# A transformer block on one core: the down projections of chunks 0 and 1 as one Strassen pair

## Chip, cores and metric

The kernel runs on one core of one Trainium2 chip. The metric is the device time of the whole kernel in microseconds, from inputs in DRAM to the output in DRAM. A core has a matrix engine (TensorE, "PE" in the profile), VectorE ("DVE"), ScalarE ("ACT"), GpSimd ("POOL"), and a queue engine that issues most transfers (SyncE, "SP"). Matmul results land in PSUM, from where VectorE or ScalarE copies them out.

## What is computed

The input x has 2048 rows of 1024. A pre-norm block with sliding, dilated attention is followed by a pre-norm block with a bilinear feed-forward of width 3584. All weights and the output are bfloat16.

```
h  = x + A(layernorm(x))
out = h + B(layernorm(h))

A(y): q, k, v = split(y @ wqkv)              # 32 heads of 32
      logits[s, w] = q[s] . k[s - 2w] / sqrt(32),  w = 0..7, masked where s - 2w < 0
      o = softmax(logits) weighted sum of v[s - 2w]
      return o @ wo
B(y): g = y @ w_gate;  u = y @ w_up          # 1024 -> 3584
      return (g * u) @ w_down                # 3584 -> 1024
```

## The kernel before

The 2048 rows are handled in four chunks of 512. First come q, k and v of all chunks. The attention itself runs on VectorE, as a background generator whose steps are laid between the other work: a step's instruction is placed when the estimated time of the matmuls has paid for it. Attention output goes through DRAM to be turned around (`oD` to `od` to `oT`), then the output projection `wo`, the second norm and the feed-forward follow.

Chunks 2 and 3 already share Strassen products: their gate/up in pair blocks, and their down projection with the four quarters of a 1024 x 3584 by 3584 x 1024 product (two chunks by two halves of the features, two halves of the features by two halves of the columns). Strassen's form takes seven block products in place of eight, with sums of blocks in float16, and needs the values scaled: a power of two from a sum of absolute values of all of a tensor ("row sums", taken on ScalarE and totalled by one small matmul).

Before the change chunk 0's down projection is a plain one, and chunk 1's is a Strassen product by itself, its rows halved (256 rows per block):

```python
psum = ctx.enter_context(tc.tile_pool(name="psum", bufs=8, space=PSUM))   # eight banks, in turn
...
def ffn2(c, hf, hT, hs, between={}):                                      # chunk 0, plain
    acc = [psum.tile([128, 512], F32, tag="mm", ...) for t in range(4)]
    for b in range(4):
        for j in range(7):
            f = b * 7 + j
            for t in range(4):
                nc.tensor.matmul(acc[t][:], lhsT=hT[f][:, bass.ts(t, 128)], rhs=wts["wd", c, hf, b][:, j, :], ...)
            if c == 0:
                abs_sum_down(hf, b, j)          # row sum of 128x512 down weights, on ScalarE
            bg.step(0.86)                        # lets the attention go on
...
def dprod(ps, q, lhs, rhs, fresh, lo=0, n=TC):                             # 14 matmuls
    for k in range(NP):
        nc.tensor.matmul(ps[...], lhsT=lhs[k][:, bass.ts(q, 128)], rhs=rhs[k][...], ...)
...
nxt = wo_ln2(0)                  # output projection and norm of chunk 0
qkv(3, range(4, 6), last=True)   # v of chunk 3
start_attention(3)
lnT2, hs = nxt
hT = ffn1(0, lnT2)               # gate/up of chunk 0: 7 blocks of 8 groups
bg.finish(atts[1])
nxt = wo_ln2(1)                  # output projection and norm of chunk 1 (norm on VectorE)
for hf in range(2):
    ffn2(0, hf, hT, hs)
lnT2, hs = nxt
hT = ffn1(1, lnT2, ...)          # gate/up of chunk 1
... # chunk 1's down projection: seven products of two dprods (28 matmuls), wo of chunks 2 and 3 between them
... # 14 pair blocks: gate/up of chunks 2 and 3; then their down projection
```

In `ffn1` a group is eight matmuls into one bank; ScalarE copies gate (`gs`) and up (`us`) out of PSUM, VectorE multiplies them, ScalarE takes row sums:

```python
mm_group(pg, wts["wg", c, b], j, lnT);  nc.scalar.copy(gs[:], pg[:]);  bg.step(GROUP_US)
mm_group(pu, wts["wu", c, b], j, lnT);  nc.scalar.copy(us[:], pu[:])
nc.vector.tensor_tensor(gs[:], gs[:], us[:], ALU.mult)
abs_sum(c, b, j)
```

At the end of one chunk's attention, GpSimd's queue moves the output:

```python
nc.gpsimd.dma_start(od[c].rearrange("c g d s -> (c g) d s"), oD[:])
oT = att.tile([128, KO, 4, SUB], BF, tag="oT", name=f"oT{c}")
for cp in range(4):
    nc.gpsimd.dma_start(oT[:, :, cp, :], od[c][cp].rearrange("(hg hl) d s -> (hl d) hg s", hl=4))
```

Of the kernel before, what the change touches and what calls it, by code (L numbers as in the profile page):

```python
# [78 lines left out]
def kernel(  # L79
# [41 lines left out]

    bg = Background()
# [13 lines left out]
    def stream_wd(c, hf):  # L136
        for b in range(4):
            stream.append((("wd", c, hf, b), wd_v[:, bass.ts(b, 7), bass.ts(hf, 512)], 7))

    NH = NF // 4  # L140
    for c in range(2):
        stream_wo(c)
        if c > 0:
            stream_wd(0, 0)
            stream_wd(0, 1)
        for b in range(7):
            stream.append((("wg", c, b), wg_v[:, :, bass.ts(b, 512)], KO))
            stream.append((("wu", c, b), wu_v[:, :, bass.ts(b, 512)], KO))
    def stream_down(name, e, hf, halves):
        for a in halves:  # L150
            stream.append((("dn", name, a), wd_e[e][:, bass.ts(a, 7), bass.ts(hf, 512)], 7))

    stream_down("21", 1, 0, (0, 1))
    stream_down("11", 0, 0, (0, 1))
    stream_wo(2)
    stream_down("12", 0, 1, (0,))
# [100 lines left out]
    class NormOnScalar(Norm1):  # L257

        def sums(self):
            room = small.tile([128, 4, 4], F32, tag="nroom", name=f"nroom{self.c}")  # L260
            self.s, self.nm, self.ss, self.nb = (room[:, i, :] for i in range(4))
            junk = lnp.tile([128, D], BF, tag="ln", name=f"njunk{self.c}")
            xs = xtiles[self.c]
            for t in range(4):
                nc.scalar.activation(junk[:], xs[t][:], ACTF.Copy, accum_out=self.s[:, t:t + 1])
                yield "later", GROUP_US
            nc.scalar.activation(self.nm, self.s, ACTF.Copy, scale=-1.0 / D)
            for t in range(4):
                nc.scalar.activation(junk[:], xs[t][:], ACTF.Square, bias=self.nm[:, t:t + 1],
                                     accum_out=self.ss[:, t:t + 1])  # L270
                yield "later", GROUP_US
# [4 lines left out]

        def rows(self):
            for t in range(4):
                ln = lnp.tile([128, D], BF, tag="ln", name=f"ln{self.c}_{t}")
                nc.scalar.activation(ln[:], xtiles[self.c][t][:], ACTF.Identity, bias=self.nb[:, t:t + 1],  # L280
                                     scale=self.rs4[:, t:t + 1])
                self.lns[t] = ln
                self.transpose(t)
                yield "later", GROUP_US
# [158 lines left out]

    def attention(c):
        qD, kD = qkv_in["q", c], qkv_in["k", c]
        lg = att.tile([128, W, SUB], F32, tag="lg", name=f"lg{c}")
        for wp in range(W // 2):
# [14 lines left out]
            yield 1.0  # L462
        if c == 0:
            nc.vector.tensor_tensor(lg[0:32, :, 0:16], lg[0:32, :, 0:16], mask[:], ALU.add)
# [54 lines left out]
    def wo_ln2(c):  # L519
# [8 lines left out]
        for t in range(4):  # L528
            for hf in range(2):
# [12 lines left out]
                bg.spend(0.7)  # L542
                bg.step(GROUP_US)
        norm(3)
        retire(2)
        return lnT, hs
# [35 lines left out]
    scale_gu, scale_d, scale_h = Scale("gu", 56), Scale("d", 56), Scale("h", 56)  # L582
    scale_h1 = Scale("h1", 28)

    def abs_sum(c, b, j):
        wt = wts["wg" if c == 0 else "wu", c, b]
        junk = lnp.tile([128, 2, 512], BF, tag="ln", name=f"junk{c}_{b}_{j}")
        scale_gu.add(28 * c + 4 * b + j, wt[:, bass.ts(j, 2), :], junk[:])

    def abs_sum_down(hf, b, j):  # L590
        junk = lnp.tile([128, 512], BF, tag="ln", name=f"junkd{hf}_{b}_{j}")
        scale_d.add(28 * hf + 7 * b + j, wts["wd", 0, hf, b][:, j, :], junk[:])
# [5 lines left out]
    def abs_sum_h1(f, ht):  # L598
        junk = lnp.tile([128, TC], BF, tag="ln", name=f"junke{f}")
        scale_h1.add(f, ht[:], junk[:])  # L600

    def ffn1(c, lnT, at={}):
        hT = []
        for b in range(7):
            if b == 5 and c + 1 < NCH:
                hss[c + 1] = load_x(c + 1, "h", nc.sync)
            for j in range(4):
                pg = psum.tile([128, TC], F32, tag="mm", name=f"pg{c}_{b}_{j}")
                mm_group(pg, wts["wg", c, b], j, lnT)
                gs = t1k.tile([128, TC], BF, tag="t1k", name=f"gs{c}_{b}_{j}")  # L610
                nc.scalar.copy(gs[:], pg[:])  # L611
                bg.step(GROUP_US)
                pu = psum.tile([128, TC], F32, tag="mm", name=f"pu{c}_{b}_{j}")
                mm_group(pu, wts["wu", c, b], j, lnT)
                us = t1k.tile([128, TC], BF, tag="t1k", name=f"us{c}_{b}_{j}")
                nc.scalar.copy(us[:], pu[:])  # L616
                nc.vector.tensor_tensor(gs[:], gs[:], us[:], ALU.mult)  # L617
                abs_sum(c, b, j)
                bg.spend(0.45)
                bg.step(GROUP_US)  # L620
                hT.append(gs)
                if (b, j) in at:
                    at[b, j]()
                f = len(hT) - 3
                if c == 1 and f >= 0:
                    abs_sum_h1(f, hT[f])
# [3 lines left out]
        if c == 1:  # L630
            for f in range(NF - 2, NF):
                abs_sum_h1(f, hT[f])
        return hT

    def ffn2_store(c, t, hf, acc, hs, lo=0, n=512):
        cols = bass.ds(hf * 512 + lo, n)
        nc.vector.tensor_tensor(hs[t][:, cols], acc[:], hs[t][:, cols], ALU.add)
# [520 lines left out]
```

## Time and profile before

| | |
|---|---|
| time, median of three runs | 776.8 us (776.63 to 778.61) |
| profiled span | 775.2 us |
| granted TensorE clock | 1.00 |
| TensorE / VectorE / ScalarE / GpSimd busy | 769.3 / 605.3 / 484.0 / 142.1 us |
| moved by DMA | 134.38 MB, mean 173 GB/s |
| stages by TensorE's clock | q, k, v to 163.6; wo of chunk 0 to 177.4; v of chunk 3 to 191.2; gate/up 0 to 287.9; wo of chunk 1 to 301.7; down 0 to 350.0; gate/up 1 to 446.8; down 1 with wo of 2 and 3 to 516.8; pair blocks and the last down projection to 775.2 |

How to read it: the page gives each engine's busy time, its busy share in 40 slices of the span (one digit each, tenths), the chain of waits followed back from the last instruction, and groups of instructions with their mean durations. Answers of the trace give timelines (start and length in us, then engine, source line, operation, output and inputs, and in brackets how long the engine stood idle before it and what ended that) and the waits of one engine. A matmul's duration in the trace overlaps the next one's; from start to start is what counts.

### The profile page before, as it was taken

To read this page: it belongs to the slowest core of one execution; us is meant where nothing else is said; L and a number is where in the kernel's file an instruction comes from. 1 tells how busy PE (TensorE), PEld (TensorE's weight loads), DVE (VectorE), ACT (ScalarE), POOL (GpSimd) and SP (SyncE) were. 2 spreads that over 40 slices of the span, in tenths; PEclk is the share of its full clock that TensorE was granted. 3 is DMA by queue.
4 is the path that set the end of the run, shared out by engine and by line. 5 is a ranking of instruction groups with operands and counts; after the bars stand their busy time and mean duration, and the time that the engine had idled before them with its cause. 6 is when DMAs were issued, how large, how long until landed. Compare 5 with 4: busy or idle time off the path is not lost.

```text
span 775.2 us, 10420 instructions
## 1 busy us (share of the span) xinstructions
PE 769.3 (99%) x3691; PEld 353.5 (46%) x3691; DVE 605.3 (78%) x766; ACT 484.0 (62%) x1040; POOL 142.1 (18%) x152
## 2 busy tenths in 40 slices
PE   8999999999999999999999999999999999999998
PEld 6444444444444444444444444444444444444444
DVE  5639999999999989999979859985553444578863
ACT  4639564322866662965777899746677776788240
POOL 0000000200002000011000001008778687600000
PEclk9999999999999999999999999999999999999999
DMA  8998896997947964978445592644332423740001
GB/s 278 265 260 199 157 230 151 299 271 224 310 133 236 308 235 125 288 257 277 142 143 192 182 299 68 157 98 114 109 95 69 109 59 106 240 140 28 0 28 55
DMA packets 183716, 134.38 MB, mean 173 GB/s; under 512 B 81264, under 2 KB 176496, under 8 KB 181616
## 3 DMA queue, kind: packets, MB, share of 16 engines
q1 hardware_dynamic: 176912, 110.12, 50.9%
q0 software_dynamic: 3584, 22.02, 8.9%
q10 hardware_dynamic: 3168, 1.57, 0.8%
q8 instruction: 29, 0.48, 0.3%
q14 instruction: 23, 0.19, 0.1%
HBM read 104.86 MB, written 22.02 MB: 164 GB/s over the span
## 4 chain that ended last, share of the span: by engine, by line
PE 93%; DVE 3%; DMA 2%; ACT 1%; issue 0%; ACTq 0%; DVEq 0%
PE ps L411 20%; PE pg L411 12%; PE pu L411 12%; PE dx L807 6%; PE pz L700 6%; PE acc L646 6%; PE py L700 6%; PE px L700 6%; PE wo L532 4%; PE wo L852 4%; PE pv L700 3%; PE dy L807 3%; PE ex L807 2%; DMA lnT<-lnr 1%; DMA w_qkv<-in_A_wqkv_dram 1%; PE ps L372 1%
## 5 line engine op out<-in xcount | busy, mean ns | idle before, releaser
L411 PE MATMUL ps<-lnT,w_qkv 128*128 128x512 bf16 x736 | 159.5, 379 | 0.0
L411 PEld LDWEIGHTS <-w_qkv 128*128 128x128 bf16 x736 | 71.9, 98 | 86.2
L411 PE MATMUL pu<-lnT,w_wu 128*128 128x512 bf16 x448 | 105.8, 379 | 0.0
L411 PE MATMUL pg<-lnT,w_wg 128*128 128x512 bf16 x448 | 105.8, 379 | 0.0
L324 ACT CAST sg<-ps 128x512 bf16<-128x512 f32 x96 | 55.2, 585 | 52.3 <-PE ps L411 49.2
L451 DVE TENSOR_TENSOR prod<-qD,kD 128x4096 bf16<-128x4096 bf16 x32 | 72.4, 2285 | 12.8 <-DMA kD<-kd 12.7
L494 DVE TENSOR_TENSOR pv<-vD,at 128x4096 bf16<-128x4096 bf16 x32 | 72.5, 2285 | 0.3
L700 PEld LDWEIGHTS <-sw 128*128 128x128 f16 x448 | 43.8, 98 | 53.8 <-issue 1.2
L411 PEld LDWEIGHTS <-w_wu 128*128 128x128 bf16 x448 | 43.8, 98 | 52.9
L411 PEld LDWEIGHTS <-w_wg 128*128 128x128 bf16 x448 | 43.7, 98 | 52.8
L616 ACT CAST us<-pu 128x512 bf16<-128x512 f32 x56 | 33.0, 590 | 43.0 <-PE pu L411 41.8
L700 PE MATMUL px<-lnT,ws 128*128 128x512 bf16 x224 | 55.2, 379 | 0.0
L700 PEld LDWEIGHTS <-ws 128*128 128x128 f16 x336 | 32.9, 98 | 39.7
L506 POOL DMA_DIRECT2D od<-oD x4 | 2.2, 542 | 264.3 <-DVE oD L504 264.3
L646 PE MATMUL acc<-w_wd,gs 128*128 128x512 bf16 x224 | 48.5, 379 | 0.0
L681 POOL TENSOR_TENSOR sw<-ws 128x512 f16<-128x512 f16 x26 | 30.0, 1152 | 85.1 <-PE py L700 77.8
L611 ACT CAST gs<-pg 128x512 bf16<-128x512 f32 x56 | 32.6, 583 | 12.9 <-PE pg L411 10.6
L453 DVE TENSOR_TENSOR prod<-prod 128x4096 bf16<-128x4096 bf16 x16 | 36.6, 2289 | 0.4
L560 ACT ACTIVATE junkd<-w_wd 128x512 bf16<-128x512 bf16 x56 | 34.3, 613 | 0.0
L646 PEld LDWEIGHTS <-gs 128*128 128x128 bf16 x224 | 21.9, 98 | 26.4
L617 DVE TENSOR_TENSOR gs<-gs,us 128x512 bf16<-128x512 bf16 x56 | 23.5, 419 | 12.5 <-ACT us L616 12.5
L185 ACT ACTIVATE rs<-mv,eps 128x1 f32<-128x1 f32 (+1 forms) x21 | 6.2, 297 | 42.0 <-DVE mv L182 36.6
(321 smaller groups left out, 1391.5 us busy)
## 6 DMA issues: line engine op xcount, KB each, us to landing
w_wg<-in_B_w_gate_dram SPq DMA_DIRECT2D x14, 1024.0 KB, 6.7
w_wu<-in_B_w_up_dram SPq DMA_DIRECT2D x14, 1024.0 KB, 5.4
w_wd<-in_B_w_down_dram SPq DMA_DIRECT2D x8, 896.0 KB, 6.2
w_pair<-in_B_w_gate_dram SPq DMA_DIRECT2D x14, 512.0 KB, 4.0
w_pair<-in_B_w_up_dram SPq DMA_DIRECT2D x14, 512.0 KB, 5.2
w_wo<-in_A_wo_dram SPq DMA_DIRECT2D x6, 1024.0 KB, 6.2
w_qkv<-in_A_wqkv_dram SPq DMA_DIRECT2D x5, 1024.0 KB, 11.0
kd<-sg SPq DMA_DIRECT2D x32, 144.0 KB, 3.3
```

What stands on the lines that cost most here:

```text
L324: nc.scalar.copy(sg[:, HB:HB + TC], ps[:])
L411: nc.tensor.matmul(ps[:], lhsT=wt[:, ko, bass.ts(j, 128)], rhs=rhs[:, ko, :], start=(ko == 0), stop=(ko == KO - 1))
L451: nc.vector.tensor_tensor(prod[:, j], qD[:], kD[:, :, o:o + SUB], ALU.mult)
L453: nc.vector.tensor_tensor(prod[:, :, 0:16], prod[:, :, 0:16], prod[:, :, 16:32], ALU.add)
L494: nc.vector.tensor_tensor(pv[:, j], vD[:, :, o:o + SUB], at[:, w, None, :].to_broadcast((128, DH, SUB)), ALU.mult)
L532: nc.tensor.matmul(ps[:], lhsT=oTs[c][:, kk, t, :], rhs=wts["wo", c, hf][:, kk, :], start=(kk == 0), stop=(kk == KO - 1))
L560: nc.scalar.activation(junk, src, ACTF.Abs, accum_out=self.l1[:, k:k + 1])
L611: nc.scalar.copy(gs[:], pg[:])
L616: nc.scalar.copy(us[:], pu[:])
L646: nc.tensor.matmul(acc[t][:], lhsT=hT[f][:, bass.ts(t, 128)], rhs=wts["wd", c, hf, b][:, j, :], start=(f == 0), stop=(f == NF - 1))
L700: nc.tensor.matmul(ps[:], lhsT=lhs[:, ko, :], rhs=rhs[:, ko, :], start=(fresh and ko == 0), stop=(ko == 3), skip_group_check=not fresh)
L807: nc.tensor.matmul(ps[:, bass.ds(lo, n)], lhsT=lhs[k][:, bass.ts(q, 128)], rhs=rhs[k][:, bass.ds(lo, n)], start=(fresh and k == 0), stop=( ...
```

## The change

Chunks 0 and 1 get the form that chunks 2 and 3 have: one Strassen pair, 512 rows per block, seven products of four `dprod`s each. It is for saving one eighth of the plain product's matmuls. Around that, four things move.

Gate-times-up of both chunks must be there first, and does not fit in SBUF twice: chunk 0's stays, chunk 1's goes to DRAM through a small ring and is read back. The same is done with the residual rows. The output projection of chunk 1 moves from after chunk 0's gate/up into it, after four of its seven blocks, and its norm goes from VectorE to ScalarE. The row sums of the down weights, which were taken while chunk 0's plain product had them in SBUF, are taken during q, k, v: quarters of one tile as a ring, loaded by ScalarE's own queue. The row sums of gate and up weights are taken 2048 elements at a time instead of 1024.

```diff
+    def abs_down():                              # row sums of the down weights
+        ring = wpool.tile([128, KO, 512], BF, tag="w", name="w_ring")
+        ...
+        def load(p):
+            nc.scalar.dma_start(rows_of(p), wd_v[:, bass.ts(p % NP, 2), bass.ts(p // NP, 512)])
+        for p in range(4):
+            load(p)
+        yield "later", 12.0
+        for p in range(NF):                      # 28
+            junk = lnp.tile([128, 2, 512], BF, tag="ln", name=f"junkd{p}")
+            scale_d.add(p, rows_of(p), junk[:])
+            if p + 4 < NF:
+                load(p + 4)
+            yield "later", 2 * GROUP_US
+        retire()
...
     qkv(0, range(4, 6))
     load_v(0)
     bg.add(norm1[3].rows(), bg.now, first=True)
+    sums = abs_down()
+    bg.add(sums, bg.now + next(sums)[1], first=True)
...
-    bg.rate = 0.98
+    bg.rate = 1.0
     nxt = wo_ln2(0)
     qkv(3, range(4, 6), last=True)
     start_attention(3)
-    lnT2, hs = nxt
-    hT = ffn1(0, lnT2)
-    bg.finish(atts[1])
-    nxt = wo_ln2(1)
-    for hf in range(2):
-        ffn2(0, hf, hT, hs)
-    lnT2, hs = nxt
+    def wo_1():
+        bg.finish(atts[1])
+        n = wo_norm(1)                           # output projection, row sums on ScalarE
+        norm2.append(n)
+        norm2.append(n.finish())                 # deviations, normalised rows, transposes
+        bg.add(norm2[1], bg.now, first=True)
+
+    bg.finish(sums)                              # what is left of the 28 sums
+    hT0 = ffn1_first(nxt[0], {4: wo_1})          # before block 4
+    bg.finish(norm2[1])
+    ffn1_second(norm2[0].lnT, {})                # to DRAM (hd1) through the ring
...
-    (chunk 1's seven products with 256-row blocks, two dprods each)
+    for q in range(4):
+        dprod(xs[q], q, A11, cells_of(b11, NH), True)        # product 1
+        if q < 2:
+            pull(1)                                          # one step of attention 3
+        if q == 1:
+            scale_d.total(ys[2])
+            scale_h1.total(ys[3])
+        ...
+            seed(0)                                          # ys = xs * scales, on VectorE
+    ...
+    for q in range(4):
+        dprod(xs[q], q, A12, cells_of(b21, NH), False)       # product 2
+        put(0, q, 0, ...)
+    ...
+    wo_adds(2, {...})                                        # wo of chunk 2, sums of blocks between
+    for q in range(4): dprod(ev, q, FS1, fcells(b11), True)      # product 3
+    for q in range(4): dprod(ys[q], q, F11, fcells(t2), False)   # product 4
+    for _ in atts[3]: pass                                       # rest of attention 3
+    for q in range(4): dprod(ys[q], q, F12, fcells(b22), False)  # product 5
+    wo_adds(3, {...})                                            # wo of chunk 3
+    for q in range(4): dprod(zs[q], q, F11, fcells(b12), False)  # product 6
+    for q in range(4): dprod(zs[q], q, F22, fcells(t4), False)   # product 7
```

The pair blocks of chunks 2 and 3 and their down projection stay as they are, up to which tiles hold the results.

## Prediction

> **What bounds the kernel now.** I read the busy shares and the chain of waits first, then TensorE's own waits, then the chain in order of time for the stages that the change rebuilds, and last the timelines of ScalarE, VectorE and GpSimd around the points where the new order puts a wait.
>
> ```profile
> PE 769.3 (99%) x3691; PEld 353.5 (46%) x3691; DVE 605.3 (78%) x766; ACT 484.0 (62%) x1040; POOL 142.1 (18%) x152
> ...
> DVE  5639999999999989999979859985553444578863
> ...
> PE 93%; DVE 3%; DMA 2%; ACT 1%; issue 0%; ACTq 0%; DVEq 0%
> ```
>
> TensorE is busy in 99% of the span and carries 93% of the chain, so a matmul taken away is time taken away, and a wait of TensorE is time added. VectorE's row is 9 in nearly every slice from the third to the twenty-first (58 to 407 us): there it has nothing left to catch up with, and whatever delays it is handed on.
>
> ```profile
> PE warm_ps L318 <- DVE warm L304: 1.2, 1, 1.2
> PE pv L700 <- DVE h L812: 0.6, 2, 0.4
> ```
>
> TensorE's waits (total, times, longest): only the start and 0.6 us later on. All there is to win is therefore the matmuls themselves, and all there is to lose are new waits.
>
> ```profile
> 287.88 13.81 PE wo L532 x64
> 301.69 48.35 PE acc L646 x224
> ...
> 446.76 6.04 PE ex L807 x28
> ```
>
> The chain in order of time (start, length, what): chunk 1's output projection, chunk 0's down projection as 224 plain matmuls, and one of the seven products of chunk 1's Strassen form, 28 matmuls.
>
> **What the Trainium skill says.** "TensorE: Matmul & The Clock Gate", section "Step-by-step: what each phase is for", gives about 216 ns from one 512-column matmul to the next in a stream; here 48.35 / 224 = 215.8 ns and 6.04 / 28 = 215.7 ns. It agrees, so matmuls can be counted. "PSUM — Partial Sum Buffer", "Specifications (TRN2)", gives 8 banks of 512 float32, so the kernel's pool of eight tiles is all of PSUM: the ninth group after any group waits until that one has been copied out. The same page, "Engine vs sequencer instructions", calls the queues of ScalarE and VectorE strictly first in, first out; the timeline below shows it, finished products waiting behind an Exp. "ScalarE: Activation LUTs", "What ACT_TABLE_LOAD costs", gives 186 ns + 0.833 ns per element without pointer operands: 1039 ns for 1024, against 1060 in the trace.
>
> **The change, part by part.**
>
> *Matmuls.* Removed: 224 of chunk 0 (48.35 us) and 7 x 28 of chunk 1 (7 x 6.04 = 42.3). Added: seven products of the pair at 56 matmuls, 7 x 56 x 0.2158 = 84.6. The balance is 90.65 - 84.6 = **6.0 us**, 28 matmuls; the instruction order of the changed kernel has exactly 28 fewer. The gain cannot be larger, since TensorE waited for nothing else. It is 0.8% of 776.8.
>
> *Row sums of the down weights.* 56 sums of 512 in the plain projection go; 28 of 1024 come during q, k, v, with their own 7.3 MB by ScalarE's queue. One sum costs about 1.05 us from start to start (198.21 to 199.26 in ScalarE's timeline). The work is even smaller than before, but where it stands matters. In the changed order 20 sums are spread among the copies of q, k and v; the last eight stand in one block between chunk 3's last v copy and the first gate copy, and one more shortly before.
>
> ```profile
> 193.97 1.06 ACT L471 ACTIVATE lg<-lg 128x1024 f32<-128x1024 f32 x1 [4.61 <-DVE lg L470]
> 194.94 0.56 ACT L324 CAST sg<-ps 128x512 bf16<-128x512 f32 x1
> ...
> 197.25 0.61 ACT L611 CAST gs<-pg 128x512 bf16<-128x512 f32 x1
> ```
>
> ScalarE, before: the Exp waits for VectorE, four v copies follow, and the first gate product, finished by TensorE at 192.9, is copied at 197.25. Nine sums put 9 x 1.05 = 9.5 us ahead of it, 206.7; the last four also need ring slots freed by sums 20 to 23, so their loads leave no earlier than about 200 to 203 and take some 4 to 5 us (256 KB loads here have medians of 4.8 to 7.3). I put the first gate copy at 208.5. The ninth group from there needs its bank and would start at 191.2 + 8 x 1.727 = 205.0: **wait A, about 4 us** (209.0).
>
> *Chunk 1's output projection moves ahead.* It ran at 287.9; now it runs after four of seven gate/up blocks, 32 x 1.727 = 55.3 us after 191.2, at **246.5**. It needs chunk 1's attention output, transposed through DRAM.
>
> ```profile
> 203.23 0.42 DVE L617 TENSOR_TENSOR gs<-gs,us 128x512 bf16<-128x512 bf16 x1
> ...
> 233.59 2.28 DVE L504 TENSOR_TENSOR oD<-oD,pv 128x4096 bf16<-128x4096 bf16 x1
> ```
>
> ```profile
> 236.17 0.54 POOL L506 DMA_DIRECT2D od<-oD  x1 [62.50 <-DVE oD L504]
> 245.09 3.54 POOL L509 DMA_DIRECT2D oT<-od  x4 [8.39 <-PE pg L411]
> ```
>
> VectorE ends that attention at 235.9, its store lands 8.2 us later, and four loads leave from 245.1 at 0.89 us each, landing 3.7 to 8.5 us after issue. So even before, the first quarter could not be there until about 249. In the changed order the first gate-up product stands after an attention add that VectorE reaches at 205.5, but its input is copied only at 209.5: VectorE idles 4 us and ends attention 1 near 240.4. With 6.8 us for the store (between the 5.3 median of such stores and the 8.2 of this one), 0.9 to issue and 5 to land, the first quarter is there at 253.5. TensorE, already 4 us late, waits a further 3: **A and B together 253.5 - 246.5 = 7.0 us**.
>
> *Chunk 1's norm on ScalarE.* VectorE loses four statistics and four normalisations, about 7.5 us; ScalarE gains 4 x (1.05 + 1.15 + 1.15) + 1.5 = 15 us. By its spacing (0.48 for a copy, 0.60 for a 512 sum, and for a 2048 sum, which no instruction here has, an estimate from the ScalarE page of 1.89) a gate/up pair costs ScalarE 2.5 of 3.45 us, and in the blocks after the projection the norm brings it near its limit. I count a lag of some 6 us, under the 12 to 13 that the banks allow: no wait of TensorE, but about 4 us that VectorE loses waiting for up copies. The transposed rows are there about 10 us before chunk 1's gate/up.
>
> *The pair's product.* At its start the scale must be known. With T the end of gate/up: last copy T+0.6, product T+1.2, sum T+2.3, row sums T+2.9, two attention multiplies T+7.4, scale T+9.3, first seeding T+10. TensorE wants the row sums at T+6.3 and the seeds at T+12.5, a margin of 2.5 to 3.4. A VectorE lag of 4 us eats it: **1.5 us**. After that VectorE has 69 us of work, by my sum over its instructions, for the next 74 us of TensorE, part of it on blocks that are still being loaded; TensorE wants the last attention output at about T+77, which VectorE finishes some 12 us earlier, about the time of a store and a load. I allow **1 us** for these together.
>
> *Transfers.* Gate-times-up of chunk 1 goes out (3.7 MB) and comes back (5.5 MB), residual rows 1.5 MB each way, one down quarter again 1.8 MB: some 14 MB on 134, at 173 GB/s mean. They delay others at the edges, but none stands on the path by its own volume.
>
> *Sum.* 776.8 - 6.0 + 7.0 + 1.5 + 1.0 = **780.3 us**.
>
> **The rivals.** *The gain arrives whole.* If the ring's loads land fast, and chunk 1's attention store takes 5.3 us and not 8.2, A and B shrink to about 3.5 together, and the pair's margins hold: 774. For it speaks how closely the author has placed the remaining attention steps; against it the 245.1 of the loads' issue against the 246.5 at which they are needed. *VectorE becomes the bound.* It is at 93% in the pair, and every lag from earlier is carried there; if seeds, converted blocks and the last attention output each come late, five or six waits of 2 to 4 us would make 790 to 797. Against it: VectorE lost 7.5 us of norm and 4.9 of output adds. *The first loads of the ring delay attention 0.* Its v load (issued 84.3, median 11.1 to land) has 6.5 us before it is wanted at 101.9; 1 MB of ring loads costs about that. Then all of VectorE moves by 1 to 3 us: 782 to 784.
>
> **Range and chances.** The gain is certain to 0.1 us; the waits are not. A plus B lies between 3.5 and 10, the rest between 0 and 8: 772 to 788 for 8 in 10. Faster by 2% would need 761.3, which 6 us cannot give; slower by 2% needs 792.5, 22 us of new waits, for which the second rival must come true.
>
> **What would show it.** In the profile after: TensorE with 3663 matmuls and a busy time shorter by up to 6; among its waits one for ScalarE's gate copy near 205 to 209 (A) and one of the output projection for the transposed attention output near 250 (B), together about 7; a short one at the row-sum matmul or the seeding near 411; the ScalarE timeline with eight sums in a row before the first gate copy. The prediction is wrong if attention 1's output lies ready when TensorE asks for it, if there are waits of 3 us or more inside the pair, or if the last pair blocks and the final products, which don't change, take another time.

## The result and the profile after

The changed kernel takes **788.7 us** (median; 787.6 to 792.5), the kernel before 776.8 beside it: a ratio of 1.0157, 95% interval 1.012 to 1.0194. It is 12 us slower where 3.5 were predicted, and lies 0.7 us above the predicted range. That it stays within 2% was foreseen; the loss is more than three times the predicted one.

The page after, busy times, VectorE's row and the chain by engine:

```profile
PE 765.5 (97%) x3607; PEld 352.0 (45%) x3663; DVE 608.4 (77%) x722; ACT 509.0 (65%) x981; POOL 142.2 (18%) x152
...
DVE  5529999999589997999999997985544534478853
...
PE 43%; DVE 42%; issue 5%; DMA 5%; ACT 4%; ACTq 1%; SPq 0%; DVEq 0%; POOLq 0%
```

3663 weight loads stand for 3663 matmuls (some matmul records are missing), 28 fewer than the 3691 before, as counted. But the chain, 93% TensorE before, is 43%: it now runs back through VectorE, transfers and ScalarE, and the eleventh slice of VectorE's row (197 to 216 us) has fallen to 5, where before had 9. TensorE's waits (total, times, longest us) name what came in between:

```profile
PE pg L430 <- ACT gs L702: 8.7, 1, 8.7
PE wo L592 <- DMA w_wo<-in_A_wo_dram: 3.0, 1, 3.0
...
PE ps L430 <- ACT halo L348: 1.0, 1, 1.0
```

The first is wait A of the prediction, at twice its size. The second, chunk 0's output projection waiting for the second half of its weights, was not in the prediction. Wait B, for chunk 1's attention output, is missing. Groups by line and shape (busy us, mean ns of one, idle before) show a loss that no wait contains:

```profile
L592 PE MATMUL wo<-w_wo,oT 128*128 128x512 bf16 x63 | 15.8, 412 | 3.0 <-DMA w_wo<-in_A_wo_dram 3.0
L568 PE MATMUL wo<-w_wo,oT 128*128 128x512 bf16 x63 | 13.9, 379 | 0.1
```

The same output projection takes 379 ns a matmul in chunk 1 and 412 in chunk 0, right after the wait. Windows of 2 us around the two waits (stretch, length, busy us and counts of TensorE, its weight loads, VectorE, ScalarE and GpSimd, then granted clock, DMA share, GB/s):

```profile
169.00:171.00 2.00, 1.92 (x6) 0.78 (x7) 1.93 (x4) 0.00 (x1) 0.00 (x0) 0.64 1.11 303
171.00:173.00 2.00, 2.00 (x6) 0.70 (x5) 2.00 (x2) 0.69 (x2) 0.00 (x0) 0.51 1.05 351
173.00:175.00 2.00, 1.95 (x10) 0.91 (x10) 2.00 (x2) 0.00 (x0) 0.00 (x0) 1.00 1.15 336
...
221.00:223.00 2.00, 2.00 (x6) 0.73 (x5) 2.00 (x3) 2.00 (x4) 0.00 (x0) 0.50 1.08 381
223.00:225.00 2.00, 2.00 (x8) 0.82 (x7) 2.00 (x2) 2.00 (x6) 0.00 (x0) 0.71 1.08 384
```

After each of the two waits TensorE is busy all the time and does 6 matmuls in 2 us instead of 9 to 11, at clock 0.5. From start to start this cost 13.79 - 56 x 0.2158 = 1.7 us after the first wait and 5.83 - 16 x 0.2158 = 2.4 us after the second.

The spans of the two profiles, 775.2 and 786.7, differ by 11.5: -6.0 (28 matmuls) + 8.7 + 3.0 + 1.0 (waits) + 4.1 (half clock) = 10.8; the remaining 0.7 arises in the pair, whose stretch with the two output projections (415.08 to 528.71) is 1.4 us longer than its 520 matmuls at 215.8 ns. From the first pair block of chunks 2 and 3 to the end both kernels take the same, 258.4 us before and 258.0 after.

**Where A comes from.** ScalarE's timeline after (start, length, line, operation; in brackets the idle time before and what ended it):

```profile
201.50 0.59 ACT L343 CAST sg<-ps 128x512 bf16<-128x512 f32 x1
...
204.36 0.40 ACTq L662 DMA_DIRECT2D w_ring<-in_B_w_down_dram  x1
204.81 1.06 ACT L625 ACTIVATE junkd<-w_ring 128x1024 bf16<-128x1024 bf16 x1 [1.57 <-DMA hsd<-h]
...
212.00 0.38 ACTq L662 DMA_DIRECT2D w_ring<-in_B_w_down_dram  x1
212.42 1.06 ACT L625 ACTIVATE junkd<-w_ring 128x1024 bf16<-128x1024 bf16 x1 [3.20 <-DMA w_wg<-in_B_w_gate_dram]
...
217.65 1.06 ACT L625 ACTIVATE junkd<-w_ring 128x1024 bf16<-128x1024 bf16 x1 [2.00 <-DMA w_ring<-in_B_w_down_dram]
...
218.70 0.57 ACT L702 CAST gs<-pg 128x512 bf16<-128x512 f32 x1
```

The last v copy starts at 201.50, the first gate copy at 218.70. Between them stand eight sums, as predicted; the ninth comes shortly before, at 199.25. Eight times 1.05 is 8.4 us. Most of the rest of the 17.2 is ScalarE standing still, 7.7 us in all: 1.1 and 2.8 at two loads of the ring, 2.0 for rows that have not landed, and 1.8 in which four loads are issued. At 209.2 it comes to a load of the ring (a DMA issue in its own queue) and stops until 212.00, when a gate weight that SyncE had ordered lands. The chain in order of time says the same:

```profile
204.26 7.66 DMA w_wg<-in_B_w_gate_dram
212.00 5.63 DMA w_ring<-in_B_w_down_dram
219.32 3.57 PE pg L430 x8
```

The two transfers have no data in common. The built program's list of instructions shows the link: transfers of both queues take turns at eight completion semaphores (counters by which a transfer reports that it has landed), and each of the 28 loads of the ring carries a wait for the earlier transfer that used its semaphore, 26 of them a transfer of SyncE's queue. In this trace ScalarE works off its queue in order, so copies and sums whose data lie ready wait behind it.

**Where VectorE was late.** The Exp ahead of the last v copies starts at 197.13 instead of 193.97. That delay is much older; ScalarE's timeline near 30 us, before and then after:

```profile
29.70 2.76 ACTq L229 DMA_TRANSPOSE lnT<-ln  x2
```

```profile
29.39 6.39 ACTq L231 DMA_TRANSPOSE lnT<-ln  x2
35.82 0.29 ACT L187 ACTIVATE rs<-mv,eps 128x1 f32<-128x1 f32 x1 [6.33 <-issue]
```

Two transposing transfers of chunk 1's first norm, which the change does not touch, take 3.6 us longer to issue. The first attention then starts at 55.17 and not at 52.02, 26 us before the ring's first load, and VectorE carries those 3.1 us on to this Exp.

### The profile page after: what moved, and what is told of

Read it like the earlier page. It is cut to its first block, busy times and chain, and to the rows that moved or that the text cites. A ratio compares the mean times of both kernels' runs of the same rounds, so it can differ in the third digit from the quotient of the medians.

```text
span 786.7 us, 10235 instructions
## 1 busy us (share of the span) xinstructions
PE 765.5 (97%) x3607; PEld 352.0 (45%) x3663; DVE 608.4 (77%) x722; ACT 509.0 (65%) x981; POOL 142.2 (18%) x152
## 4 chain that ended last, share of the span: by engine, by line
PE 43%; DVE 42%; issue 5%; DMA 5%; ACT 4%; ACTq 1%; SPq 0%; DVEq 0%; POOLq 0%
DVE prod L472 7%; PE dx L916 6%; PE pz L800 6%; PE py L800 6%; PE px L800 6%; DVE pv L516 6%; DVE prod L474 3%; PE pv L800 3%; PE ey L916 3%; PE pg L430 3%; PE dy L916 3%; PE pu L430 3%; DVE pv L524 2%; DVE t L479 2%; DVE st L183 2%
## 5 line engine op out<-in xcount | busy, mean ns | idle before, releaser
L472 DVE TENSOR_TENSOR prod<-qD,kD 128x4096 bf16<-128x4096 bf16 x32 | 72.3, 2285 | 13.9 <-DMA kD<-kd 13.8
L430 PE MATMUL pg<-lnT,w_wg 128*128 128x512 bf16 x221 | 54.3, 388 | 8.8 <-ACT gs L702 8.7
L800 PE MATMUL px<-lnT,ws 128*128 128x512 bf16 x212 | 53.1, 379 | 0.6
L430 PE MATMUL pu<-lnT,w_wu 128*128 128x512 bf16 x218 | 53.2, 383 | 0.3
L430 PE MATMUL pwg<-lnT,w_wg 128*128 128x512 bf16 x220 | 52.5, 379 | 0.2
L430 PE MATMUL pwu<-lnT,w_wu 128*128 128x512 bf16 x219 | 52.5, 379 | 0.3
L916 PEld LDWEIGHTS <-gs 128*128 128x128 f16 (+1 forms) x280 | 27.4, 98 | 33.4 <-issue 0.5
L625 ACT ACTIVATE junkd<-w_ring 128x1024 bf16<-128x1024 bf16 x28 | 29.8, 1063 | 7.7 <-DMA w_wg<-in_B_w_gate_dram 3.2
L817 ACT COPY py<-px 128x512 f32<-128x512 f32 x28 | 16.0, 570 | 28.5 <-PE px L800 28.5
L782 POOL TENSOR_TENSOR sw<-sw,ws 128x512 f16<-128x512 f16 x26 | 30.0, 1155 | 2.0
L784 POOL TENSOR_TENSOR sw<-ws,sw 128x512 f16<-128x512 f16 x26 | 30.2, 1162 | 0.0
```

What stands on the lines that cost most here:

```text
L430: nc.tensor.matmul(ps[:], lhsT=wt[:, ko, bass.ts(j, 128)], rhs=rhs[:, ko, :], start=(ko == 0), stop=(ko == KO - 1))
L472: nc.vector.tensor_tensor(prod[:, j], qD[:], kD[:, :, o:o + SUB], ALU.mult)
L625: nc.scalar.activation(junk, src, ACTF.Abs, accum_out=self.l1[:, k:k + 1])
L782: eng.tensor_tensor(sw[:, i, 1], sw[:, i, 0], a11, ALU.subtract)
L784: eng.tensor_tensor(sw[:, i, 3], a12, sw[:, i, 1], ALU.subtract)
L800: nc.tensor.matmul(ps[:], lhsT=lhs[:, ko, :], rhs=rhs[:, ko, :], start=(fresh and ko == 0), stop=(ko == 3), skip_group_check=not fresh)
```

## The experiments

| Kernel | Median us | Ratio to before, 95% interval |
|---|---|---|
| changed | 788.73 | 1.0157, 1.012 to 1.0194 |
| e3: no down row sums, no ring | 778.02 | 1.0006, 0.9992 to 1.0019 |
| e5: sums without loads | 779.88 | 1.0046, 1.0029 to 1.0063 |
| e6: loads without sums | 782.87 | 1.0076, 1.0061 to 1.0091 |
| e1: eight sums in the output projection | 783.43 | 1.0072, 1.0046 to 1.0099 |
| e2: output weights early | 793.29 | 1.0196, 1.0156 to 1.0237 |
| e4: e1 and e2 | 790.49 | 1.0156, 1.011 to 1.0202 |
| e8: ring by GpSimd's queue | 786.91 | 1.0116, 1.009 to 1.0141 |
| e9: e8 and e1 | 783.80 | 1.0078, 1.0054 to 1.0103 |
| e10: e9, wo of chunk 1 3.5 us later | 786.55 | 1.0118, 1.0103 to 1.0133 |
| e12: e8, sums closer together | 783.09 | 1.0083, 1.0062 to 1.0104 |
| e13: changed, sums closer together | 786.04 | 1.0157, 1.0082 to 1.0232 |
| e7: e3, wo of chunk 1 a block later | 786.98 | 1.0123, 1.0106 to 1.0139 |
| e14: e3, wo of chunk 1 3.5 us later | 780.50 | 1.0044, 1.0029 to 1.0059 |
| e15: e3, two transposes on TensorE | 774.24 | 0.9964, 0.995 to 0.9978 |
| e16: changed, two transposes on TensorE | 787.32 | 1.0135, 1.01 to 1.017 |
| e17: ring early | 779.78 | 1.0033, 1.002 to 1.0046 |
| e18: e17, output weights early | 784.40 | 1.0081, 1.0067 to 1.0096 |

The ratios are to the executions of the kernel before taken beside each run. Of e13 and of e16 one execution (801.6 and 799.9 us) counts as slow and is left out here and below. e11 is the kernel before with ScalarE held by extra sums (832.0, one execution).

### The ring taken apart: e3, e5, e6

**e3** leaves out the down row sums and all loads of the ring.

```diff
-    sums = abs_down()
-    bg.add(sums, bg.now + next(sums)[1], first=True)
+    nc.vector.memset(scale_d.l1[:], 100.0)
...
-    bg.finish(sums)
```

Expected: 

> Leaves out the row sums of the down weights and their 7.3 MB of loads altogether; the scale is made from a constant. All else as changed. Theory (the ring is the whole of the loss): no wait for the gate copy, none for the output weights, 770.8 plus what the attention output of chunk 1 makes TensorE wait at 246.5: about 3 us and 2 us at half clock if it is at hand at 249.5, so 771 to 776. Rival (the pair and the norm have a cost of their own, hidden so far behind the 8.7 us wait): waits near 411 and in the pair, 778 to 784.

Measured: 778.0, with executions from 773.4 to 782.1, where the kernel before stays within 2 us. In its profile (774.8, one of the quick ones) TensorE never waits longer than 1.2 us. So A and the wait for the output weights belong to the ring; but most executions are 1 to 6 us longer than the one profiled, so that the median lies above the theory's 771 to 776, and this run cannot say why (e15 does).

**e5** fills the ring's four quarters once and sums them seven times over, so ScalarE's work stays and 24 of 28 loads go.

```diff
-            if p + 4 < NF:
-                load(p + 4)
             yield "later", 2 * GROUP_US
```

Expected: 

> Leaves out 24 of the 28 loads of the ring: its four quarters are filled once and summed seven times over, so the scale is made from other sums; ScalarE's 28 sums stand where they stood. Theory (what held ScalarE were the ring's loads in its queue, each of which waits for an unrelated earlier transfer, not the sums): the wait for the first gate copy shrinks from 8.7 us to the 3 to 4 us that nine sums in a row cost, 779 to 783. Rival (the sums are the cost): it stays at 7 to 9 us, 786 to 789.

Measured: 779.9. TensorE's waits:

```profile
PE pg L430 <- ACT gs L700: 2.8, 1, 2.8
PE wo L568 <- DMA oT<-od: 2.1, 1, 2.1
PE pg L430 <- ACT sg L346: 1.4, 1, 1.4
```

The sums alone make A 2.8 us, a little less than the theory's 3 to 4, and with A small the wait B appears, 2.1. The wait for the output weights is gone although the ring still holds its buffer.

**e6** keeps the loads and cuts each sum to 8 columns.

```diff
-            scale_d.add(p, rows_of(p), junk[:])
+            scale_d.add(p, rows_of(p)[:, :, 0:4], junk[:, :, 0:4])
```

Expected: 

> Leaves out nearly all of each sum: 2 x 4 columns of every quarter are summed instead of 1024, so the scale is made from other sums; the 28 loads, their place in ScalarE's queue and what they wait for stay. Theory (the loads hold ScalarE): the wait for the first gate copy stays 4 to 8 us and ScalarE stands still for 2 to 9 us at several loads in q, k, v: 783 to 789. Rival (the sums are the cost): no wait for the gate copy, 776 to 780.

Measured: 782.9 (the theory had 783 to 789), the wait for the gate copy 5.0 us with hardly any work ahead of it. ScalarE's timeline at one load in q, k, v:

```profile
157.76 0.21 ACT L625 ACTIVATE junkd<-w_ring 128x8 bf16<-128x8 bf16 x1
157.87 0.19 ACT L625 ACTIVATION_READ_ACCUMULATOR junkd<-w_ring 128x1 f32 x1
163.22 0.45 ACTq L662 DMA_DIRECT2D w_ring<-in_B_w_down_dram  x1
163.71 0.59 ACT L343 CAST sg<-ps 128x512 bf16<-128x512 f32 x1 [5.65 <-DMA qd<-sg]
```

A sum of 0.21 us, and then ScalarE stands for over 5 us until a store of q has landed, with a q product waiting to be copied. The loads, not the sums, are the larger cost: over e3 the sums alone cost 1.9 us (e5), the loads alone 4.9 (e6), both together 10.7, so each makes the other dearer.

### Other places for the ring: e1, e2, e4, e8, e9, e12, e13

**e1** pulls eight sums into chunk 0's output projection, where ScalarE idles, so that none is left for the block.

```diff
-    nxt = wo_ln2(0)
+    nxt = wo_ln2(0, {k: lambda: next(sums, None) for k in range(8)})
```

Expected: 

> Eight of the 28 down row sums are pulled forward into chunk 0's output projection, where ScalarE idles; the block of eight ahead of the first gate copy is gone. Theory (the block is what held TensorE): the 8.7 us wait and its 2.4 us at half clock go, 788.7 - 11.1 = 777.6; TensorE then asks for chunk 1's attention output at about 252, which VectorE, no longer held for 11 us, has ready at 251 to 254, so a wait of 0 to 2 us: 777 to 781. Rival (the sums and their transfers cost the same wherever they stand): the wait moves to the norm of chunk 0 or to the gate weights, 785 to 790.

Measured: 783.4. A is gone, as the theory said; in its place, in the quickest execution, which is the profiled one (780.5), come 2.6 us for the transposed norm of chunk 0, 2.2 for the output weights, 1.9 for chunk 1's attention output, 1.6 for a copy. Over the expected 777 to 781: half of what A had cost came back as other waits.

**e2** loads the second half of chunk 0's output weights earlier, into the buffer of a dead normalised chunk; **e4** does this and e1.

```diff
-    stream_wo(0)
+    stream.append((("wo", 0, 0), wo_v[:, :, bass.ts(0, 512)], KO))
...
+    wts["wo", 0, 1] = lnTp.tile([128, KO, 512], BF, tag="lnT", name="w_wo_0_1")
+    nc.sync.dma_start(wts["wo", 0, 1][:], wo_v[:, :, bass.ts(1, 512)])
     qkv(3, range(4), last=True)
```

Expected of e2: 

> The second half of chunk 0's output weights gets a buffer of its own (a dead normalised chunk's) and is loaded when chunk 3's q, k, v begin; the ring and the block of eight sums stay. Theory (the ring's buffer delayed this load): the 3.0 us wait near 166 and its 2.0 us at half clock go; the wait for the gate copy stays 8 to 11 us. 783.6 if the ring's last loads come earlier by as much, 786 to 788 if they don't. Rival (the load is late because the transfers are saturated, not for lack of a buffer): the wait stays, 788 to 789.

Expected of e4: 

> The eight sums in the output projection and the output weights early, together. Theory: the two gains add, 788.7 - 11.1 - 5.0 = 772.6, plus a wait for chunk 1's attention output that now shows, 0 to 5 us with its half clock: 772 to 778, within 2 us of the kernel without the sums. Rival (one bottleneck, the transfers): no better than the better of the two alone, 778 or more.

Measured: 793.3 and 790.5, both above their theories; e4's rival (778 or more) came true. In e2's profile (796.4, its longest execution) the wait for the weights is gone and A is 7.1, but ScalarE is stopped 13.0 us at a load of the ring near 104 by a transposing transfer, and TensorE waits 11.2 for its copy. The moved load is asked for only at 160.98, so that stop is not its effect, and what the early weights alone are worth stays open. In e4 TensorE waits 7.0 us for the transposed norm of chunk 0, where e1 has 2.6, and still 1.7 for the first half of the output weights, asked for at 159.35.

**e8** issues the ring's loads from GpSimd's queue; **e9** does so and pulls the eight sums as e1.

```diff
-            nc.scalar.dma_start(rows_of(p), wd_v[...])
+            nc.gpsimd.dma_start(rows_of(p), wd_v[...])
```

Expected of e8: 

> The 28 loads of the ring are issued from GpSimd's queue; the sums and everything else stay as changed. Theory (loads in ScalarE's in-order queue): ScalarE is never stopped by a load, no wait for its copies of q, k, v, and the wait for the first gate copy is the 3 to 5 us of nine sums in a row: 779 to 784. Rival (the transfers are saturated, so the sums wait for their rows whoever issues): 786 to 790.

Expected of e9: 

> The ring's loads from GpSimd's queue and eight sums pulled into chunk 0's output projection, together: nothing in ScalarE's queue waits for a load's turn, and no sums stand in a block ahead of the first gate copy. Theory (the loss is the block, its loads' landing of 4 to 7 us, and ScalarE stopped at loads): no wait for the gate copy, none for the output weights, 0 to 2 us for the transposed norm of chunk 0 and 0 to 3 us for chunk 1's attention output: 772 to 777. Rival (7.3 MB more on saturated transfers delay something else by as much): 780 or more.

Measured: 786.9 and 783.8. In e8 the stops in q, k, v and the wait for output weights are gone, but A is 9.9 us: in the block ScalarE waits 3.1 and 5.0 us for rows of the ring whose loads left at 199 and 201, once slots were free, and landed 7 and 11 us later. The rival (786 to 790) was right. In e9, too, the rival's 780 or more came true: A is gone, but TensorE waits 5.4 us for the transposed norm of chunk 0, whose transposes now share 177 to 191 with the ring's last loads (DMA share 0.96 there against 0.70 before).

**e12** is e8 with the sums closer together, **e13** the same with loads in ScalarE's queue.

```diff
-            yield "later", 2 * GROUP_US
+            yield "later", 0.99 * (1 + (p % 3 == 2)) * GROUP_US
```

Expected of e12: 

> The ring's loads from GpSimd's queue, and the sums spaced by one or two groups (three sums in four groups) instead of two, so that the last is done three groups before chunk 0's output projection; none stands in a block, and no load of the ring falls into 165 to 210, where weights, transposes and v stores fill the transfers. Theory (the ring costs time only where it meets that stretch or stops ScalarE): no wait for gate copy, output weights or chunk 0's transposed norm; what is left is chunk 1's attention output, 0 to 3 us: 771 to 776. Rival (7.3 MB more in q, k, v delay the attention's own transfers wherever they lie): 778 to 784.

Expected of e13: 

> The same faster spacing with the loads in ScalarE's queue as in the changed kernel; one line differs from it. Theory (ScalarE is stopped at a load until an earlier transfer has landed): the block ahead of the first gate copy is gone, but stops of 2 to 10 us at loads in q, k, v remain, now closer together: one or two waits of TensorE for q, k, v copies, 776 to 783. Rival (only where the sums stand matters): as with GpSimd's queue, 771 to 776.

Measured: 783.1 and 786.0 (785.3 to 796.9). e12 missed its 771 to 776 and lies in its rival's range; e13 lies above both of its own. In e12 GpSimd's queue works in order too, and a sum of ScalarE waits for loads that stand behind another tensor's store; GpSimd's timeline, then ScalarE's:

```profile
139.80 0.58 POOL L528 DMA_DIRECT2D od<-oD  x1
145.70 3.52 POOL L531 DMA_DIRECT2D oT<-od  x4 [5.32 <-DMA od<-oD]
149.21 0.56 POOL L456 DMA_DIRECT2D vD<-vd  x1
149.76 2.11 POOL L662 DMA_DIRECT2D w_ring<-in_B_w_down_dram  x3
```

```profile
159.49 1.06 ACT L625 ACTIVATE junkd<-w_ring 128x1024 bf16<-128x1024 bf16 x1 [11.91 <-DMA w_ring<-in_B_w_down_dram]
```

Three loads, whose slots came free between 140 and 145, leave at 149.8, after chunk 0's attention output has been stored and reloaded. ScalarE is held 11.9 us and TensorE 5.8. In e13 the same stretch stops ScalarE for 5.1 us at a load and TensorE for 4.9.

### Chunk 1's output projection: e7, e10, e14

**e7** is e3 with the projection after five of seven blocks; **e14** is e3, **e10** e9, with it a quarter into the fifth block.

```diff
-    hT0 = ffn1_first(nxt[0], {4: wo_1})
+    hT0 = ffn1_first(nxt[0], {5: wo_1})        # e7;  {(4, 1): wo_1} in e10 and e14
```

Expected of e7: 

> As the kernel without the down row sums and their loads (left out, the scale made from a constant), with chunk 1's output projection after five of seven gate and up blocks and not after four: 13.8 us later. Theory (without the ring, chunk 1's attention output is asked for at 247.3 with next to no margin, and that is where its executions differ, 773 to 782): 771 to 773.5 in all executions. Rival (the spread comes from elsewhere, or the later norm now delays chunk 1's gate and up): 774 to 782 as before.

Expected of e14: 

> Leaves out the down row sums and their loads as before (scale from a constant), and starts chunk 1's output projection 3.5 us later, a quarter into the fifth block. Theory (without the ring the executions differ by 773 to 782 because chunk 1's attention output comes 0 to 5 us late, and over 3 us a half clock is added): 772 to 775 with a spread under 3 us. Rival (the spread comes from elsewhere): 774 to 782 as with the projection at the block's start.

Expected of e10: 

> As the one before, and chunk 1's output projection starts a quarter into the fifth gate and up block, 3.5 us later. Theory (its input comes 0 to 3 us late after four blocks, and the norm behind it has about 4 us to spare, since 13.8 us later cost 9.8): the wait for the attention output goes and none for the norm comes, 771.5 to 774, with less spread. Rival (the norm on ScalarE has no room): a wait of 1 to 4 us for its transposed rows ahead of chunk 1's gate and up, 774 to 778.

Measured: 787.0, 780.5 and 786.6, none better than with four blocks; all three theories fell, and e14's rival (774 to 782) held. TensorE's longest wait in e7, then in e14:

```profile
PE pwg L430 <- DMA lnT<-ln: 9.8, 1, 9.8
```

```profile
PE pg L430 <- ACT gs L702: 2.5, 1, 2.5
```

13.8 us later costs 9.8 at chunk 1's gate and up, so with four blocks the transposed norm is there some 4 us ahead of need, not the 10 that the prediction gave it. In e14 the norm loads ScalarE so late in the gate and up blocks that a gate copy is 2.5 us late, and the row-sum matmuls wait 1.7. e10 has no such gate wait and none for the attention output, but 1.6 us at the row sums, 6.7 for chunk 0's transposed norm (5.4 in e9) and 1.5 for the output weights. Of the three places tried, four blocks is the best. An earlier one was not tried.

### The clock after a wait: e11

The kernel before, with ScalarE held by 11 to 16 extra sums at the start of six gate and up blocks.

```diff
+            for i in range(hold.get((c, b), 0)):
+                junk = lnp.tile([128, 2, 512], BF, tag="ln", name=f"hold{c}_{b}_{i}")
+                nc.scalar.activation(junk[:], wts["wg", c, b][:, 0:2, :], ACTF.Abs, accum_out=probe[:])
```

Expected: 

> The kernel before, with ScalarE held by extra sums of 1024 columns of resident weights at the start of six gate and up blocks: 12, 14, 16 of them in blocks 1, 3, 5 of chunk 0, and 11, 13, 15 in those of chunk 1. TensorE gets waits of different lengths with nothing else changed. Theory (half clock for about 4 us follows a wait of 3 us or more and none a wait of 2.8 or less, as the waits so far showed): each wait over 3 us is followed by 4 to 4.5 us at clock 0.5, a loss of 2 to 2.3 us whatever its length. Rival (the loss grows with the wait): a wait of 5 us or more costs clearly more than one of 3.

TensorE's timeline at three of the waits (in brackets), 8 matmuls each:

```profile
221.27 3.57 PE L411 MATMUL pg<-lnT,w_wg 128*128 128x512 bf16 x8 [2.42 <-ACT gs L617]
...
402.69 1.89 PE L411 MATMUL pg<-lnT,w_wg 128*128 128x512 bf16 x8 [1.85 <-ACT gs L617]
...
445.54 3.57 PE L411 MATMUL pg<-lnT,w_wg 128*128 128x512 bf16 x8 [13.72 <-ACT gs L617]
```

After 2.42, 4.78, 7.14, 8.56 and 13.72 us the next group takes 1.6 us longer and the one after it 0 to 0.5: a loss of 1.6 to 2.2, whatever the wait's length, and none after 1.85 us. The other runs widen the range: 1.4 us after 5.8 (e12), 2.9 after 6.7, 7.0 and 7.1 (e10, e4, e2), 1.7 after 9.8 (e7). That the loss does not grow with the wait is shown; why it varies is not, and the limit of 3 us was not right. Waits of 2.65, 2.81 (e1, e5) and 3.19 us (e16) were followed by full speed, 2.46 (e14) and 2.96 (the changed kernel) by the slow clock, so between 2.4 and 3.2 us it goes either way.

### The spread, and the ring early: e15 to e18

**e15** is e3 with the last two row tiles of chunk 1's first norm transposed on TensorE like the first two, not by two transfers in ScalarE's queue; **e16** is the changed kernel with the same edit.

```diff
             if t > 1 and on_array:
-                if t < 4:
+                if t < 6:
                     n.transpose_on_array(t - 2)
```

Expected of e15: 

> Leaves out the down row sums and their loads (scale from a constant), and transposes the last two row tiles of chunk 1's first norm on TensorE as the first two already are, instead of by two transfers in ScalarE's queue. In the profiles so far those two transfers hold ScalarE 2.7 us (before, and the quickest execution without the ring) or 6.2 to 8.1 us (the changed kernel and most others), and the first attention starts about 3 us later with the long ones. Theory (this chance makes the two groups of executions, 774 and 778): TensorE gets 1 to 2 us more work, every execution lies within 2 us, near 774 to 776. Rival (the spread is from chunk 1's attention output or the transfers in general): median 777 to 780, spread 5 us or more.

Expected of e16: 

> The changed kernel, nothing left out, with only those two transposes moved to TensorE. Theory (the long transfers in ScalarE's queue are 3 us of VectorE's lateness, which moves the Exp ahead of the block of sums and so the first gate copy): the wait for the gate copy shrinks from 8.7 to 5 to 6 us, 784 to 787. Rival (the ring alone sets that wait): 788 to 790.

Measured, e15: 774.24, all five executions between 774.19 and 774.26. e3's spread of 9 us is gone with these two transfers. In the profiles they hold ScalarE 2.7 us in the kernel before and e11, in e3's quick execution, e8 and e9, and 6.2 to 8.1 us in the others; why the same instructions take longer in the new program was not found. TensorE's waits in e15:

```profile
PE ey L635 <- DVE rowbh L630: 1.0, 1, 1.0
PE pv L800 <- DVE hsr L758: 0.7, 1, 0.7
...
PE ey L635 <- DVE rowbd L630: 0.3, 1, 0.3
PE ex L914 <- DVE ey L964: 0.3, 1, 0.3
```

This is the pair without the ring's disturbance: 1.6 us of waits at its start, and 0.7 in the first pair block of chunks 2 and 3 behind it, where before had 0.6. Waits A and B and the one for the norm are absent.

e16: 787.3 (784.5 to 790.6), at the edge of the theory's 784 to 787, but with an interval that overlaps that of the changed kernel. In its profile, the quickest execution, A is 6.2 us where 5 to 6 were expected. That the long issue enlarges A is supported by this one profile, that it matters for the median is not. The spread stays: with the ring in place executions differ by 6 us without those two transfers.

**e17** starts the ring before chunk 0's v, loads it by GpSimd's queue, and runs one sum a group, with the transposes of e15; all loads stand ahead of chunk 0's attention output. **e18** adds the early output weights of e2.

```diff
+    sums = abs_down()                          # ahead of this line, not after it
+    bg.add(sums, bg.now + next(sums)[1], first=True)
     qkv(0, range(4, 6))
...
-            yield "later", 2 * GROUP_US
+            yield "later", 0.99 * GROUP_US
```

Expected of e17: 

> Nothing left out: the ring starts before chunk 0's v and its loads go by GpSimd's queue, the sums run at most one a group, so that all 28 loads and sums are done before chunk 0's attention output goes out near 137; the two transposes on TensorE. Theory (the ring costs time only where it meets the stretch from 140 to 210 or stops ScalarE): no wait for gate copy, output weights or transposed norm, 774 to 777, at or under the kernel before. Rival (then it delays the first attention's v load, and with it all of VectorE): waits for chunk 1's attention output or near 411, 778 to 784.

Expected of e18: 

> As the run before (ring early and by GpSimd's queue, sums done before chunk 0's attention output leaves, two transposes on TensorE, nothing left out), and the second half of chunk 0's output weights in the buffer of a dead normalised chunk, asked for ahead of chunk 3's stores. Theory: its 2.2 us wait for these weights goes, nothing else is added: 774 to 777, at or a little under the kernel before. Rival (another transfer then comes late in the same stretch, as when this was tried with the ring in place): 778 to 783 with a wait for the transposed norm.

Measured: 779.8 and 784.4. e17's waits (beside 1.0 at the row sums as in e15):

```profile
PE wo L592 <- DMA w_wo<-in_A_wo_dram: 2.2, 1, 2.2
...
PE ps L430 <- ACT halo L348: 0.9, 1, 0.9
PE pg L430 <- DMA lnT<-ln: 0.9, 1, 0.9
```

No wait over 2.2 us and no slow clock in this profile, one of the quickest executions (778.0; 777.8 to 782.3); e17 is the best placing of the complete change, and 9 us better than the changed kernel, but above the expected 774 to 777 and 0.3% slower than before. e18 removes the 2.2 and meets 4.8 us for the transposed norm, as its rival said, and 4.3 for a copy; this last one lies at 106, before the moved load is asked for at 151.65, and its cause is open. No run sends the ring's loads by SyncE's queue. No complete version beats the kernel before; e15, which does by 2.9 us, leaves the row sums out.

## Why the prediction was wrong, step by step

**The gain, 6.0 us: right.** 28 matmuls fewer. e15 is 2.9 us faster than before. Its profiled span is 2.7 shorter: 6.0 less 2.7 by which the pair exceeds its matmuls more than before (1.6 of it the waits at its start), less 0.8 by which TensorE is later ahead of the pair, where the added transposes stand, plus 0.2 from the rest.

**Wait A, 4 us: mechanism right, size wrong.** The failed step is "I put the first gate copy at 208.5". Its nine sums were right in number and cost (e5: 2.8 us of wait from sums alone). Its loads "leave no earlier than about 200 to 203 and take some 4 to 5 us" were wrong in kind: a load in ScalarE's queue waits for an unrelated transfer (e6: 5.0 us from loads alone), and ScalarE stood still for 7.7 us in the block. The last four left at 204.36 to 212.00 and took 5.6 to 6.4 us to land. The copy came at 218.70, 10.2 us late; 3.2 of these are the late Exp (197.13 for 193.97). TensorE was 5.5 late itself (first gate group at 196.68 for 191.2), so that 4 + 10.2 - 5.5 = 8.7.

**Wait B, 3 us: hidden, not absent.** Timelines of VectorE, GpSimd and TensorE in the changed kernel:

```profile
219.79 0.43 DVE L685 TENSOR_TENSOR gs<-gs,us 128x512 bf16<-128x512 bf16 x1 [10.99 <-ACT us L709]
...
250.20 0.54 POOL L528 DMA_DIRECT2D od<-oD  x1 [73.45 <-DVE oD L526]
258.93 3.54 POOL L531 DMA_DIRECT2D oT<-od  x4 [8.19 <-DMA od<-oD]
...
263.13 13.98 PE L568 MATMUL wo<-w_wo,oT 128*128 128x512 bf16 x63
```

VectorE, held 11 us by the same late copies, ends attention 1 at 249.9; the store of its output starts at 250.2, the loads leave from 258.93 and land from 3.9 us on, at 262.8, and TensorE asks at 263.1. By the prediction's own criterion, output ready when asked for, this step fails, by 0.3 us and because A has made TensorE late as well. With a smaller A it appears: 2.1 us in e5, 1.9 in e1; in e15, where VectorE is not held (the store starts at 235.79, the loads leave at 242.22, TensorE asks at 247.10), there is none.

**What the sum left out: the output weights, 3.0 us.** The prediction noted the ring's buffer nowhere as a cost. It holds one of seven weight buffers until the last sum, and chunk 0's output weights are asked for at 148 and 162 instead of 110 and 144; SyncE's timelines, before and then after:

```profile
109.75 0.53 SPq L167 DMA_DIRECT2D w_wo<-in_A_wo_dram  x1
...
143.94 0.70 SPq L167 DMA_DIRECT2D w_wo<-in_A_wo_dram  x1
```

```profile
148.46 7.11 SPq L169 DMA_DIRECT2D w_wo<-in_A_wo_dram  x1
...
161.63 0.87 SPq L169 DMA_DIRECT2D w_wo<-in_A_wo_dram  x1
```

e8 and e5, with the ring still in its buffer, don't have the wait, and e17, whose ring is done at 146, still asks for the second half at 161.81 and waits 2.2 us, so the buffer alone does not make it. Which share falls to the buffer and which to the traffic was not separated.

**What the sum left out: the clock, 4.1 us.** The prediction counted every wait at its own length. The page it cites for the 216 ns, "TensorE: Matmul & The Clock Gate" of the Trainium skill, says in "Part 1: The HAM clock gate (the "warmup" mystery)" that after an idle window of about 3.4 us the array runs at half clock until it has been busy about as long. The runs agree in kind: clock 0.5, a loss of 1.4 to 2.9 us after every wait of 4.3 us or more. They differ in the limit: waits of 2.42, 2.46 and 2.96 us set it off already, one of 3.19 did not. Had both of the predicted waits, 4 and 3 us, set it off at 2 us each, the prediction would have read 11 and not 7, and 784.

**Norm on ScalarE, no wait: right, with less room.** 4 us ahead and not 10 (e7). A sum of 2048, estimated at 1.89 us, takes 1.94.

**The pair, 2.5 us: near.** In e15 1.6 of waits at its start, 2.7 in all. The last pair blocks and the final products took the same time, as said.

**The rivals.** The gain arriving whole, 774, is what e15 shows once the row sums and the ring are left out. VectorE as the bound of the pair fell: no wait over 1 us there in any profile without added holds. The ring delaying attention 0's v load fell as a cause of the lateness: VectorE was 3 us late 26 us before the first load. But its thought, 7.3 MB more on transfers that have no room, was the right one for another stretch, from 140 to 210. The prediction's account of transfers (14 MB, "none stands on the path by its own volume") leaves the ring out; the sum counts its loads only as the last four ahead of the gate copy.

**Its arithmetic.** The terms given for chunk 1's first quarter (240.4, 6.8, 0.9 and 5) add up to 253.1, not 253.5. The parts of the range (3.5 to 10 and 0 to 8) give 774.3 to 788.8, not 772 to 788, and 2% slower is 792.3. VectorE's row is 9 from the fourth slice on, not the third. None of these moves the estimate by more than 0.4 us.

## What to carry to other kernels

A load placed in a compute engine's queue is an in-order wait of that engine: look in the built program for what each load waits for, not only at what it brings. Before moving work into idle time of an engine, look at the transfers of that stretch; here every placing of the 7.3 MB with their sums cost 5 us or more over the same kernel without them (e12 over e3 5.1, e17 over e15 5.5), and a wait that was taken away mostly let another one show. And add the slow clock to a long wait of TensorE: here it followed every wait of 4.3 us or more and three of six between 2.4 and 3.2, so two such waits can cost more than one of their total length.

## What the runs showed of the hardware that was not expected

The slow clock's loss does not grow with the wait: 1.4 to 2.9 us after waits from 2.4 to 13.7 us. The issue of two transposing transfers in ScalarE's queue takes 2.7 or 6.2 to 8.1 us, with nothing of it changed; in the kernel without the ring, taking these two away brought executions from a spread of 9 us to one of 0.1.
